# XCiT cross-covariance attention and a GELU feed-forward on one core: a fixed issue order with the next batch's attention between the feed-forward steps

## The chip, the cores and the metric

One Trainium2 chip, one of its cores. The time is the device time of one execution in microseconds (us). Before the change three runs gave 914.15, 913.35 and 912.41 us, a median of 913.35.

## What is computed

The reference normalises q and k of each batch over the 6080 tokens, forms a 256 x 256 matrix of scores between channels, takes the softmax of its rows, and multiplies v by it. The result goes through a feed-forward layer with a tanh GELU, without biases.

```python
B, N, C = (4, 6080, 256)          # d_ff = 2048, all inputs FP32, tau = 1
qn = q / (norm(q, axis=1) + 1e-06)
kn = k / (norm(k, axis=1) + 1e-06)
a  = softmax(kn.transpose(0, 2, 1) @ qn / tau, axis=-1)
x  = (v @ a).reshape(B * N, C)
out = gelu_tanh(x @ w_in) @ w_out
```

## The kernel before, in words

The kernel folds the attention into the first weight: for each batch it computes aw = a @ w_in (256 x 2048, in BF16) and then runs the feed-forward on v itself, so that v @ a is never formed.

A planner orders the instructions of each engine; nothing in the code fixes the order but the order of the calls and the buffers. Set up once (lines 58 to 79): an identity, ones, and w_in and w_out, loaded in FP32 on the SP queue through one staging buffer and converted on ScalarE (L72, L77). v is cast to BF16 by a DMA from DRAM to DRAM on the POOL queue, one DMA of 6080 x 256 for each batch (v_bf, L82), at the head of the batch.

For each of the four batches:

- Gram: 48 tiles of 128 tokens (the last has 64). Each loads q and k with two casting DMAs on POOL (L89, L90; six buffers qk), squares q on ScalarE (L92) and k on VectorE (L93), and adds two matmuls into G, k stationary (L97). The squares of two tiles are added on VectorE (L108), and a matmul with a column of ones sums them over the tokens into ss, one row (L109): 24 for each batch.
- The softmax chain: reciprocal and square root of ss (L118 to L121), small FP32 matmuls that spread the row over the partitions and turn it into a column (L124, L126), scaling and Exp with a row sum (L138, L139), a reciprocal, four transposes of the exponentials on TensorE with copies (L147, L153), and 16 matmuls into awps with eight evictions on ScalarE that give aw (L161, L167).
- Feed-forward, 12 blocks of 512 tokens (the last 448), 48 in all: v arrives transposed by two DMA transposes on SP (vT, L179). For each of 16 chunks of d_ff two matmuls of 512 columns give hp (L187, three buffers of one PSUM bank shared with awps), and ScalarE writes Gelu of it as g (L192). Then, for each of four groups of 128 tokens, 16 matmuls of 256 columns accumulate yp (L199), VectorE copies it out (L203), and the ACT queue stores the block (L207, L214).

The planner already puts the Gram work of a later batch among the feed-forward blocks of the present one where buffers and loads allow, and single yp matmuls between hp matmuls.

Of the kernel before, what the change touches and what calls it, by code (L numbers as in the profile page):

```python
# [2 lines left out]

# [6 lines left out]
FP32 = mybir.dt.float32  # L10
F32R = mybir.dt.float32r
BF16 = mybir.dt.bfloat16
AF = mybir.ActivationFunctionType


@with_exitstack
def kernel(
# [34 lines left out]
    gp = ctx.enter_context(tc.tile_pool(name="gp", bufs=FC + 2))
    yout = ctx.enter_context(tc.tile_pool(name="yout", bufs=3))

    pG = ctx.enter_context(tc.tile_pool(name="pG", bufs=1, space=bass.MemoryType.PSUM))
    pM = ctx.enter_context(tc.tile_pool(name="pM", bufs=1, space=bass.MemoryType.PSUM))
    pH = ctx.enter_context(tc.tile_pool(name="pH", bufs=3, space=bass.MemoryType.PSUM))
    pY = ctx.enter_context(tc.tile_pool(name="pY", bufs=2, space=bass.MemoryType.PSUM))

    ident = const.tile([128, 128], FP32)  # L60
    make_identity(nc, ident)
    ident_bf = const.tile([128, 128], BF16)
    nc.gpsimd.tensor_copy(ident_bf, ident)
    ones_col = const.tile([128, 1], BF16)
    nc.vector.memset(ones_col, 1.0)
    ones_row = const.tile([1, 128], FP32)
    nc.vector.memset(ones_row, 1.0)

    win_st = stage.tile([128, CHUNKS, D], FP32, tag="wst")
    nc.sync.dma_start(out=win_st, in_=moe_w_in.rearrange("(c p) d -> p c d", p=128))  # L70
    win_bf = const.tile([128, CHUNKS, D], BF16)
    nc.scalar.activation(win_bf, win_st, AF.Copy)  # L72

    wout_st = stage.tile([128, FC, 256], FP32, tag="wst")
    nc.sync.dma_start(out=wout_st, in_=moe_w_out.rearrange("(t p) d -> p t d", p=128))
    wout_bf = const.tile([128, FC, 256], BF16)
    nc.scalar.activation(wout_bf, wout_st, AF.Copy)  # L77

    v_bf = dram.tile([B * N, C], BF16)

# [170 lines left out]
```

## Time and profile before

| | |
|---|---|
| median of three runs | 913.35 us |
| span of the profiled execution | 913.5 us |
| TensorE matmuls (PE) busy | 804.7 us, 88% |
| ScalarE (ACT) busy | 503.3 us, 55% |
| VectorE (DVE) busy | 190.3 us, 21% |
| POOL busy | 206.5 us, 23% |
| q and k loads | 376 of 64 KB and 8 of 32 KB, 2.6 us each from issue to landing |
| v casts | 4 of 3040 KB, 20.8 us each |

Busy times overlap, so they don't add up to the span. Sizes of DMAs are those written, in BF16; the FP32 that is read is twice as much. Two matmuls in a row overlap in their recorded times, so the pitch of a run is read from the starts, not from the mean length. The granted clock is 1 at the upper of TensorE's two levels (2.4 GHz) and 0.5 at the lower (1.2 GHz).

### The profile page before, as it was taken

The page shows a single profiled execution, that of the slowest core. Times are in us where ns is not written, and L with a number is a line of the kernel's source. Part 1 is how long each engine was busy: PE and PEld are TensorE (multiplying, and loading weights), DVE is VectorE, ACT ScalarE, POOL GpSimd, SP SyncE. Part 2 cuts the span into 40 slices and gives each one's busy share as a digit, 9 for nine tenths or more (in the row PEclk, how much of TensorE's full clock was granted, in tenths as well). Part 3 has the DMA queues.
Part 4 walks back from the last instruction along what each step waited for, and adds up shares of the span by engine and source line. Part 5 has one row for each costly group of instructions (what it writes and reads, how often), then busy time and mean ns, then how long its engine had stood idle before and what let it go on. Part 6 is the DMA issues. An engine that isn't in the chain of part 4 may idle for free. (4 is left out here: it accounts for less than half of the span.)

```text
span 913.5 us, 13551 instructions
## 1 busy us (share of the span) xinstructions
PE 804.7 (88%) x5136; PEld 498.9 (55%) x5184; DVE 190.3 (21%) x518; ACT 503.3 (55%) x1031; POOL 206.5 (23%) x395
## 2 busy tenths in 40 slices
PE   0537529999999979999999889999999889999998
PEld 0101206666666637575666546575757545766666
DVE  0224302121221322121212313121212210101101
ACT  0333616565656385656566485656565466465563
POOL 2649412221212232312121222312121000000000
PEclk9995659999999989999999989999999999999999
DMA  9999984353534444534444434534443102212111
GB/s 234 232 177 122 187 155 76 82 87 76 81 80 78 85 46 76 96 72 90 73 85 74 90 36 82 92 70 93 70 92 67 55 12 58 58 56 61 46 47 44
DMA packets 134624, 79.80 MB, mean 87 GB/s; under 512 B 58784, under 2 KB 133792, under 8 KB 133792
## 3 DMA queue, kind: packets, MB, share of 16 engines
q0 software_dynamic: 55360, 37.38, 30.3%
q1 hardware_dynamic: 54048, 16.66, 8.2%
q10 hardware_dynamic: 25152, 24.91, 7.9%
q8 instruction: 40, 0.66, 0.3%
q14 instruction: 24, 0.20, 0.1%
HBM read 78.91 MB, written 37.36 MB: 127 GB/s over the span
## 5 line engine op out<-in xcount | busy, mean ns | idle before, releaser
L192 ACT ACTIVATE g<-hp 128x512 bf16<-128x512 f32 (+1 forms) x768 | 384.3, 625 | 275.2 <-PE hp L187 274.7
L199 PE MATMUL yp<-wout_bf,g 128*128 128x256 bf16 (+1 forms) x3072 | 372.8, 273 | 0.1
L187 PE MATMUL hp<-vT,aw 128*128 128x512 bf16 (+1 forms) x1492 | 368.3, 377 | 3.7 <-ACT g L192 1.3
L199 PEld LDWEIGHTS <-g 128*128 128x128 bf16 (+1 forms) x3072 | 300.4, 98 | 68.8 <-issue 0.8
L187 PEld LDWEIGHTS <-aw 128*128 128x128 bf16 x1536 | 148.7, 97 | 159.9 <-issue 35.9
L89 POOL DMA_DIRECT2D qk<-in_q_dram x192 | 111.0, 578 | 449.0 <-ACT g L192 360.9
L97 PE MATMUL G<-qk 128*128 128x256 bf16 (+1 forms) x384 | 79.2, 309 | 65.6 <-DMA qk<-in_k_dram 64.7
L203 DVE COPY ysb<-yp 128x256 f32<-128x256 f32 x192 | 81.2, 423 | 257.3 <-PE yp L199 257.1
L90 POOL DMA_DIRECT2D qk<-in_k_dram x192 | 112.6, 587 | 43.2 <-DMA v_bf<-in_v_dram 39.1
L92 ACT ACTIVATE sq<-qk 128x256 bf16<-128x256 bf16 x192 | 77.0, 455 | 76.9 <-DMA qk<-in_q_dram 54.9
L93 DVE TENSOR_TENSOR sq<-qk 128x256 bf16<-128x256 bf16 x192 | 54.9, 289 | 309.1 <-DMA qk<-in_k_dram 270.5
L97 PEld LDWEIGHTS <-qk 128*128 128x128 bf16 (+1 forms) x384 | 30.5, 101 | 118.3 <-DMA qk<-in_k_dram 94.1
L108 DVE TENSOR_TENSOR sq<-sq 128x512 bf16<-128x512 bf16 x96 | 40.7, 424 | 142.3 <-ACT sq L92 137.7
L109 PE MATMUL ss<-sq,ones_col 128*1 128x512 bf16 x96 | 41.8, 448 | 11.7 <-DVE sq L108 9.9
L167 ACT ACTIVATE aw<-awps,rsinv 128x512 bf16<-128x512 f32 x32 | 19.4, 695 | 9.7 <-PE awps L161 9.7
L161 PE MATMUL awps<-win_bf,eT 128*128 128x512 bf16 x60 | 20.5, 468 | 2.9 <-DVE eT L153 2.9
L124 PE MATMUL M<-rrow,ones_row 1*128 1x256 f32 x8 | 4.9, 710 | 19.7 <-ACT rrow L120 19.7
L109 PEld LDWEIGHTS <-ones_col 128*1 128x1 bf16 x96 | 7.7, 81 | 25.1 <-issue 24.7
L72 ACT ACTIVATE win_bf<-win_st 128x4096 bf16<-128x4096 f32 x1 | 3.6, 3618 | 20.9 <-DMA win_st<-in_moe_w_in_dram 20.9
L118 DVE RECIPROCAL inv<-ss 1x512 f32<-1x512 f32 x4 | 13.4, 3346 | 3.5 <-PE ss L109 3.5
L124 PEld LDWEIGHTS M<-rrow,ones_row 1*128 1x128 f32 x8 | 2.0, 306 | 21.2 <-ACT rrow L120 21.2
L161 PEld LDWEIGHTS <-eT 128*128 128x128 bf16 x64 | 7.1, 117 | 11.3 <-issue 5.5
(27 smaller groups left out, 47.7 us busy)
## 6 DMA issues: line engine op xcount, KB each, us to landing
out_dram<-ysb ACTq DMA_DIRECT2D x44, 512.0 KB, 2.9
v_bf<-in_v_dram POOLq DMA_DIRECT2D x4, 3040.0 KB, 20.8
qk<-in_q_dram POOLq DMA_DIRECT2D x188, 64.0 KB, 2.6
qk<-in_k_dram POOLq DMA_DIRECT2D x188, 64.0 KB, 2.6
win_st<-in_moe_w_in_dram SPq DMA_DIRECT2D x1, 2048.0 KB, 22.2
wout_st<-in_moe_w_out_dram SPq DMA_DIRECT2D x1, 2048.0 KB, 13.6
vT<-v_bf SPq DMA_TRANSPOSE x96, 2.7
out_dram<-ysb ACTq DMA_DIRECT2D x4, 384.0 KB, 2.5
```

What stands on the lines that cost most here:

```text
L89: nc.gpsimd.dma_start(out=qk[:rows, 0, :], in_=q[b, n0 : n0 + rows, :])
L90: nc.gpsimd.dma_start(out=qk[:rows, 1, :], in_=k[b, n0 : n0 + rows, :])
L92: nc.scalar.activation(sq[:rows, 0:256], qk[:rows, 0, :], AF.Square)
L93: nc.vector.tensor_mul(sq[:rows, 256:512], qk[:rows, 1, :], qk[:rows, 1, :])
L97: nc.tensor.matmul(G[:, ci, 0:256], lhsT=qk[:rows, 1, ci * 128 : ci * 128 + 128], rhs=qk[:rows, 0, :], start=first, stop=last,)
L108: nc.vector.tensor_add(sq_prev[:rows], sq_prev[:rows], sq[:rows])
L109: nc.tensor.matmul(ss, lhsT=ones_col, rhs=sq_prev, start=it <= 1, stop=last,)
L161: nc.tensor.matmul(awps, lhsT=eT[:, jc, ic * 128 : ic * 128 + 128], rhs=win_bf[:, jc, fs * 512 : fs * 512 + 512], start=jc == 0, stop=jc = ...
L187: nc.tensor.matmul(hp[:, :cols], lhsT=aw[:, cc, fc * 128 : fc * 128 + 128], rhs=vT[:, cc, :cols], start=cc == 0, stop=cc == CHUNKS - 1)
L192: nc.scalar.activation(g[:, :cols], hp[:, :cols], AF.Gelu_apprx_tanh)
L199: nc.tensor.matmul(yp[:r, 0:256], lhsT=gs[fc][:, s * 128 : s * 128 + r], rhs=wout_bf[:, fc, :], start=fc == 0, stop=fc == FC - 1)
L203: nc.vector.tensor_copy(ysb[:r, s, :], yp[:r, 0:256])
```

## The change

The body of the function is rewritten under a manual schedule: the order of the calls is the order on each engine.

- Loads of q and k take eight rows of tokens for each partition: token p x 47 + r lies on partition p, and one DMA brings rows r0 to r0 + 7 of all partitions, 8 KB in one piece for each of them (load_qk). Batch 0 has seven such chunks, the others six; the 64 tokens left over have a DMA of their own.
- Scores are computed transposed (q stationary), so that their exponentials need no transpose. Square sums of batch 0 go through TensorE with a 128 x 128 matrix of ones (ss_row, one matmul for each row); those of the others are added on VectorE (sum_rows) and summed over the partitions by one FP32 matmul (ss_total). 1/norm is Exp(-0.5 Ln(x)). The sums of the softmax come from matmuls with ones (row_sums).
- w_in and w_out are cast by DMAs on POOL, and stand behind the loads of batch 0; v of batch 0 is cast in two pieces, 1024 tokens behind the fourth pair of loads and the rest behind the weights.
- The feed-forward is software-pipelined over the 48 blocks, in eight steps: step p has four hp matmuls of block n into a pair of PSUM banks, one Gelu of 2 x 512, and eight yp matmuls of block n - 1. Between the steps of block blk of a batch stands the attention of the next batch: loads in blocks 1 to 6, one Gram row for each step in blocks 2 to 7, the cast of v in block 7, the softmax chain in block 8, the eight parts of aw in block 9, evicted by VectorE and ScalarE in turn.
- vT is requested two blocks ahead on SP, and the stores move from the ACT queue to SP.

The lines that are added, cut to the core; the ones removed are those of the kernel above. `ss_row` is `gram_row` with `ones_bf` stationary and the squares moving; `rows_of` lists a chunk's rows.

```diff
+    sqp = ctx.enter_context(tc.tile_pool(name="sqp", bufs=2))
+    vts = ctx.enter_context(tc.tile_pool(name="vts", bufs=4))
+    gp = ctx.enter_context(tc.tile_pool(name="gp", bufs=2))
+    pA = ctx.enter_context(tc.tile_pool(name="pA", bufs=2, space=bass.MemoryType.PSUM))
+    pH = ctx.enter_context(tc.tile_pool(name="pH", bufs=2, space=bass.MemoryType.PSUM))
...
+    def chunks_of(b):
+        sizes = [8, 8, 8, 8, 8, 4, 3] if b == 0 else [8, 8, 8, 8, 8, 7]
...
+    def load_qk(b, c):
+        r0, n = chunks_of(b)[c]
+        last = r0 + n == R
+        qt = qkp.tile([128, 8, 256], BF16, tag="q")
+        kt = qkp.tile([128, 8, 256], BF16, tag="k")
+        for t, src in ((qt, q), (kt, k)):
+            nc.gpsimd.dma_start(
+                out=t[:, 0:n, :],
+                in_=src[b, 0 : R * 128, :].rearrange("(p r) c -> p r c", r=R)[:, r0 : r0 + n, :])
+            if last and REM:
+                nc.gpsimd.dma_start(out=t[:REM, n, :], in_=src[b, R * 128 : N, :])
+        qk_tiles[b, c] = (qt, kt)
...
+    def cast_v(b, t0, t1):
+        nc.gpsimd.dma_start(out=v_bf[b][t0:t1, :], in_=v[b, t0:t1, :])
...
+    def squares(b, c):
+        qt, kt = qk_tiles[b, c]
+        r0, n = chunks_of(b)[c]
+        last = r0 + n == R
+        sq = sqp.tile([128, 8, 512], BF16, tag="sq")
+        if last and REM:
+            nc.gpsimd.memset(sq[:, n, :], 0.0)
+        nc.scalar.activation(sq[:, 0:n, 0:256], qt[:, 0:n, :], AF.Square)
+        nc.vector.tensor_mul(sq[:, 0:n, 256:512], kt[:, 0:n, :], kt[:, 0:n, :])
...
+        SQ[b, c] = sq
+    def sum_rows(b, c):
+        sq = SQ.pop((b, c))
+        a1 = addp.tile([128, 4, 512], BF16, tag="a1")
+        nc.vector.tensor_add(a1, sq[:, 0:4, :], sq[:, 4:8, :])
+        a2 = addp.tile([128, 2, 512], FP32, tag="a2")
+        nc.vector.tensor_add(a2, a1[:, 0:2, :], a1[:, 2:4, :])
+        if c == 0:
+            acc = accp.tile([128, 512], FP32, tag="acc")
+            ACC[b] = acc
+            nc.vector.tensor_add(acc, a2[:, 0, :], a2[:, 1, :])
+        else:
+            acc = ACC[b]
+            a3 = addp.tile([128, 512], FP32, tag="a3")
+            nc.vector.tensor_add(a3, a2[:, 0, :], a2[:, 1, :])
+            nc.vector.tensor_add(acc, acc, a3)
+    def gram_row(b, c, i):
+        if (b, c, i) == (b, 0, 0):
+            G[b] = pA.tile([128, 2, 256], FP32, tag="a", name=f"G{b}")
+        qt, kt = qk_tiles[b, c]
+        rows = rows_of(b, c)
+        r, np_ = rows[i]
+        first = c == 0 and i == 0
+        last = c == len(chunks_of(b)) - 1 and i == len(rows) - 1
+        for jc in range(2):
+            nc.tensor.matmul(
+                G[b][:, jc, :],
+                lhsT=qt[:np_, r, jc * 128 : jc * 128 + 128],
+                rhs=kt[:np_, r, :],
+                start=first and jc == 0, stop=last and jc == 1)
...
+    def ss_total(b):
+        SS[b] = pA.tile([128, 512], FP32, tag="a", name=f"ss{b}")
+        nc.tensor.matmul(SS[b], lhsT=ones_f, rhs=ACC[b], start=True, stop=True)
+    def scores(b):
+        ss = SS[b]
+        lnk = smx.tile([128, 256], FP32, tag="lnk")
+        nc.scalar.activation(lnk, ss[:, 256:512], AF.Ln, bias=eps)
+        qq = smx.tile([128, 2], FP32, tag="qq")
+        for jc in range(2):
+            junk = smx.tile([128, 128], FP32, tag="junk")
+            nc.vector.scalar_tensor_tensor(
+                junk, ss[:, jc * 128 : jc * 128 + 128], 1.0, ident,
+                op0=ALU.mult, op1=ALU.mult, accum_out=qq[:, jc : jc + 1])
+        rk = smx.tile([128, 256], FP32, tag="rk")
+        nc.scalar.activation(rk, lnk, AF.Exp, scale=-0.5)
+        lnq = smx.tile([128, 2], FP32, tag="lnq")
+        nc.scalar.activation(lnq, qq, AF.Ln, bias=eps)
+        rq = smx.tile([128, 2], FP32, tag="rq")
+        nc.scalar.activation(rq, lnq, AF.Exp, scale=-0.5, bias=log_it)
+        S = smx.tile([128, 2, 256], FP32, tag="S")
+        eT = smx.tile([128, 2, 256], BF16, tag="eT")
+        for jc in range(2):
+            nc.vector.tensor_mul(S[:, jc, :], G[b][:, jc, :], rk)
+        for jc in range(2):
+            nc.scalar.activation(eT[:, jc, :], S[:, jc, :], AF.Exp, scale=rq[:, jc : jc + 1])
+        nc.scalar.preload_act_table(AF.Gelu_apprx_tanh)
+        ET[b] = eT
+    def row_sums(b):
+        ps = pA.tile([128, 2], FP32, tag="a")
+        for ic in range(2):
+            for jc in range(2):
+                nc.tensor.matmul(ps[:, ic : ic + 1],
+                                 lhsT=ET[b][:, jc, ic * 128 : ic * 128 + 128],
+                                 rhs=ones_bf[:, 0:1], start=jc == 0, stop=jc == 1)
+        rs = smx.tile([128, 2], FP32, tag="rs")
+        nc.vector.reciprocal(rs, ps)
+        RS[b] = rs
...
+    def aw_part(b, fs, ic, eng):
+        if b not in AW:
+            AW[b] = awp.tile([128, 2, D], BF16, tag="aw", name=f"aw{b}")
+        ps = pA.tile([128, 512], FP32, tag="a")
+        for jc in range(2):
+            nc.tensor.matmul(ps, lhsT=ET[b][:, jc, ic * 128 : ic * 128 + 128],
+                             rhs=win_bf[:, jc, fs * 512 : fs * 512 + 512],
+                             start=jc == 0, stop=jc == 1)
+        o = AW[b][:, ic, fs * 512 : fs * 512 + 512]
+        if eng == "act":
+            nc.scalar.activation(o, ps, AF.Copy, scale=RS[b][:, ic : ic + 1])
+        else:
+            nc.vector.tensor_scalar_mul(o, ps, RS[b][:, ic : ic + 1])
...
+    def mm1(n, p):
+        b = n // NB
+        cols = cols_of(n)
+        if p == 0:
+            GS[n] = gp.tile([128, FC, BLK], BF16, tag="g", name=f"g{n}")
+        hp = pH.tile([128, 2, 512], FP32, tag="h")
+        for u in range(2):
+            fc = 2 * p + u
+            for cc in range(2):
+                nc.tensor.matmul(hp[:, u, :cols],
+                                 lhsT=AW[b][:, cc, fc * 128 : fc * 128 + 128],
+                                 rhs=vt_tiles[n][:, cc, :cols],
+                                 start=cc == 0, stop=cc == 1)
+        nc.scalar.activation(GS[n][:, 2 * p : 2 * p + 2, :cols], hp[:, :, :cols],
+                             AF.Gelu_apprx_tanh)
...
+    def mm2(n, p):
+        cols = cols_of(n)
+        s, half = divmod(p, 2)
+        if half == 0 and s % 2 == 0:
+            YP[n] = pY.tile([128, 2, 256], FP32, tag="y", name=f"yp{n}_{s}")
+            if s == 0:
+                YS[n] = yout.tile([128, 4, 256], FP32, tag="ysb", name=f"ysb{n}")
+        r = min(128, cols - s * 128)
+        yp = YP[n]
+        for fc in range(half * 8, half * 8 + 8):
+            nc.tensor.matmul(yp[:r, s % 2, :],
+                             lhsT=GS[n][:, fc, s * 128 : s * 128 + r],
+                             rhs=wout_bf[:, fc, :], start=fc == 0, stop=fc == FC - 1)
+        if half == 1 and s % 2 == 1:
+            ysb = YS[n]
...
+                nc.vector.tensor_copy(ysb[:, s - 1 : s + 1, :], yp)
...
+        nc.sync.dma_start(
+            out=out[r0 : r0 + nf * 128, :].rearrange("(s p) c -> p s c", p=128),
+            in_=ysb[:, 0:nf, :])
...
+        nch = len(chunks_of(0))
+        VC = 1024
+        for c in range(nch):
+            load_qk(0, c)
+            if c == 3:
+                cast_v(0, 0, VC)
+                load_vt(0)
+            squares(0, c)
+            for i in range(len(rows_of(0, c))):
+                gram_row(0, c, i)
+                ss_row(0, c, i)
+        nc.gpsimd.dma_start(out=win_bf, in_=moe_w_in.rearrange("(c p) d -> p c d", p=128))
+        nc.gpsimd.dma_start(out=wout_bf, in_=moe_w_out.rearrange("(t p) d -> p t d", p=128))
+        cast_v(0, VC, N)
+        load_vt(1)
+        scores(0)
+        row_sums(0)
+        for fs in range(2):
+            aw_part(0, fs, 0, "dve")
+            aw_part(0, fs, 1, "act")
+        NN = B * NB
+        for n in range(NN + 1):
+            b, blk = divmod(n, NB)
+            nxt = b + 1
+            for p in range(PAIRS):
+                if n < NN:
+                    if p == 0 and n + 2 < NN:
+                        load_vt(n + 2)
+                    mm1(n, p)
+                if n == 0 and p in (1, 3):
+                    fs = 2 + p // 2
+                    aw_part(0, fs, 0, "dve")
+                    aw_part(0, fs, 1, "act")
+                if n >= 1:
+                    mm2(n - 1, p)
+                    if p == PAIRS - 1:
+                        store(n - 1)
+                if n < NN and nxt < B:
+                    ncn = len(chunks_of(nxt))
+                    if p == 0 and 1 <= blk <= ncn:
+                        load_qk(nxt, blk - 1)
+                    if p == 0 and blk == ncn + 1:
+                        cast_v(nxt, 0, N)
+                    c = blk - 2
+                    if 0 <= c < ncn:
+                        if p == 0:
+                            squares(nxt, c)
+                        gram_row(nxt, c, p)
+                        if p == 4:
+                            sum_rows(nxt, c)
+                    if blk == 8:
+                        if p == 2:
+                            ss_total(nxt)
+                            scores(nxt)
+                        if p == 6:
+                            row_sums(nxt)
+                    if blk == 9:
+                        aw_part(nxt, p // 2, p % 2, "act" if p % 2 else "dve")
```

## Rows read from the trace of the kernel before

**Rows 1.** The page, busy us, share of the span and instructions of each engine.
```profile
PE 804.7 (88%) x5136; PEld 498.9 (55%) x5184; DVE 190.3 (21%) x518; ACT 503.3 (55%) x1031; POOL 206.5 (23%) x395
```
**Rows 2.** Stages: us, busy of PE, PEld, DVE, ACT, POOL, granted clock, DMA share, GB/s.
```profile
0.00:23.60 23.60, 0.00 (x0) 0.00 (x0) 0.21 (x2) 1.97 (x2) 5.57 (x16) 1.00 0.95 233
23.60:93.80 70.20, 40.41 (x120) 8.51 (x120) 23.98 (x74) 25.95 (x51) 51.21 (x98) 0.83 1.15 175
93.80:131.00 37.20, 11.20 (x44) 5.26 (x45) 7.14 (x17) 14.21 (x25) 7.51 (x15) 0.59 1.00 192
...
310.00:333.00 23.00, 16.63 (x101) 10.22 (x101) 9.64 (x22) 11.65 (x25) 5.29 (x10) 0.85 0.35 54
333.00:520.00 187.00, 185.34 (x1248) 120.44 (x1256) 40.22 (x115) 113.34 (x239) 45.56 (x86) 1.00 0.45 81
520.00:541.00 21.00, 12.95 (x57) 6.09 (x57) 7.68 (x17) 13.33 (x23) 9.36 (x18) 0.76 0.42 51
...
724.00:741.00 17.00, 9.49 (x34) 3.82 (x34) 5.31 (x9) 10.93 (x19) 0.00 (x0) 0.80 0.02 6
741.00:913.50 172.50, 168.20 (x1135) 111.52 (x1145) 20.39 (x48) 95.08 (x192) 0.00 (x0) 1.00 0.18 51
```
**Rows 3.** The chain of waits in time, last batch: start us, length us, what.
```profile
776.37 6.44 PE yp L199 x59
...
790.54 6.44 PE yp L199 x59
...
903.43 6.57 PE yp L199 x59
```
**Rows 4.** Timeline of PE, second batch: start us, length us, line, operation, count.
```profile
334.03 0.82 PE L97 MATMUL G<-qk 128*128 128x256 bf16 x6
...
353.27 1.89 PE L187 MATMUL hp<-vT,aw 128*128 128x512 bf16 x8
355.00 0.27 PE L199 MATMUL yp<-wout_bf,g 128*128 128x256 bf16 x1
355.11 2.48 PE L187 MATMUL hp<-vT,aw 128*128 128x512 bf16 x10
```
**Rows 5.** Timeline of ACT in a block of the last batch.
```profile
769.74 7.46 ACT L192 ACTIVATE g<-hp 128x512 bf16<-128x512 f32 x15
```
**Rows 6.** The page's groups: busy us, mean ns, idle before and releaser.
```profile
L192 ACT ACTIVATE g<-hp 128x512 bf16<-128x512 f32 (+1 forms) x768 | 384.3, 625 | 275.2 <-PE hp L187 274.7
...
L108 DVE TENSOR_TENSOR sq<-sq 128x512 bf16<-128x512 bf16 x96 | 40.7, 424 | 142.3 <-ACT sq L92 137.7
...
L124 PE MATMUL M<-rrow,ones_row 1*128 1x256 f32 x8 | 4.9, 710 | 19.7 <-ACT rrow L120 19.7
...
L72 ACT ACTIVATE win_bf<-win_st 128x4096 bf16<-128x4096 f32 x1 | 3.6, 3618 | 20.9 <-DMA win_st<-in_moe_w_in_dram 20.9
```
**Rows 7.** Timeline of ACT in the first softmax chain.
```profile
97.17 1.28 ACT L120 ACT_TABLE_LOAD   x1
98.46 0.41 ACT L120 ACTIVATE rrow<-inv 1x256 f32<-1x256 f32 x1
```
**Rows 8.** Timeline after the first softmax chain, with idle time before and its releaser.
```profile
103.74 2.34 PE L161 MATMUL awps<-win_bf,eT 128*128 128x512 bf16 x5 [0.72 <-DVE eT L153]
...
130.74 0.53 POOL L90 DMA_DIRECT2D qk<-in_k_dram  x1 [13.69 <-DMA v_bf<-in_v_dram]
...
131.18 1.25 PE L97 MATMUL G<-qk 128*128 128x256 bf16 x4 [19.73 <-DMA qk<-in_k_dram]
```
**Rows 9.** Timeline of POOL's DMA issues in the first batch's Gram.
```profile
42.95 0.54 POOL L82 DMA_DIRECT2D v_bf<-in_v_dram  x1 [0.24 <-DMA qk<-in_q_dram]
...
60.82 0.53 POOL L90 DMA_DIRECT2D qk<-in_k_dram  x1 [8.40 <-DMA v_bf<-in_v_dram]
...
63.48 0.57 POOL L89 DMA_DIRECT2D qk<-in_q_dram  x1
64.00 0.57 POOL L90 DMA_DIRECT2D qk<-in_k_dram  x1
```

More of the change, by code (lines that the diff above doesn't have):

```diff
@@ L2 @@
 from contextlib import ExitStack
+import math
 import concourse.bass as bass
@@ L64 @@
[L64 to L75, printed above, removed]
@@ new lines @@
+    qk_tiles = {}
+    def load_qk(b, c):
[10 more added lines that the diff above has]
+        qk_tiles[b, c] = (qt, kt)
@@ new lines, with load_vt @@
+    v_bf = {}
+    def cast_v(b, t0, t1):
+        nc.gpsimd.dma_start(out=v_bf[b][t0:t1, :], in_=v[b, t0:t1, :])
+    vt_tiles = {}
+    def load_vt(n):
+        b, blk = divmod(n, NB)
+        t0 = blk * BLK
+        cols = min(BLK, N - t0)
+        vT = vts.tile([128, 2, BLK], BF16, tag="vT")
+        for cc in range(2):
+            nc.sync.dma_start_transpose(
+                out=vT[:, cc, :cols], in_=v_bf[b][t0 : t0 + cols, cc * 128 : cc * 128 + 128])
+        vt_tiles[n] = vT
+    G, SS, ACC, SQ = {}, {}, {}, {}
@@ new lines, in rows_of @@
+    def rows_of(b, c):
+        r0, n = chunks_of(b)[c]
+        rows = [(r, 128) for r in range(n)]
+        if r0 + n == R and REM:
+            rows.append((n, REM))
+        return rows
+    def squares(b, c):
+        qt, kt = qk_tiles[b, c]
+        r0, n = chunks_of(b)[c]
+        last = r0 + n == R
[4 more added lines that the diff above has]
+        nc.vector.tensor_mul(sq[:, 0:n, 256:512], kt[:, 0:n, :], kt[:, 0:n, :])
+        if last and REM:
+            nc.scalar.activation(sq[:REM, n, 0:256], qt[:REM, n, :], AF.Square)
+            nc.vector.tensor_mul(sq[:REM, n, 256:512], kt[:REM, n, :], kt[:REM, n, :])
+        SQ[b, c] = sq
@@ new lines, in ss_row @@
+    def ss_row(b, c, i):
+        if (b, c, i) == (b, 0, 0):
+            SS[b] = pA.tile([128, 512], FP32, tag="a", name=f"ss{b}")
+        rows = rows_of(b, c)
+        r, np_ = rows[i]
+        first = c == 0 and i == 0
+        last = c == len(chunks_of(b)) - 1 and i == len(rows) - 1
+        nc.tensor.matmul(SS[b], lhsT=ones_bf[:np_, :], rhs=SQ[b, c][:np_, r, :],
+                         start=first, stop=last)
+    def ss_total(b):
+        SS[b] = pA.tile([128, 512], FP32, tag="a", name=f"ss{b}")
+        nc.tensor.matmul(SS[b], lhsT=ones_f, rhs=ACC[b], start=True, stop=True)
@@ new lines @@
+    ET, RS = {}, {}
+    def scores(b):
[22 more added lines that the diff above has]
+        ET[b] = eT
@@ new lines, with cols_of @@
+    GS = {}
+    def cols_of(n):
+        return min(BLK, N - (n % NB) * BLK)
+    def mm1(n, p):
[6 more added lines that the diff above has]
+            fc = 2 * p + u
+            for cc in range(2):
+                nc.tensor.matmul(hp[:, u, :cols],
[4 more added lines that the diff above has]
+                             AF.Gelu_apprx_tanh)
```

195 lines of the change are left out of this document (47 added, 148 removed).

## The prediction, made before the changed kernel was run

> **What bounds the kernel now.** I read four views, in this order. The page's first line says that TensorE (PE) is busy for 804.7 of 913.5 us, 88% [rows 1]; ScalarE (ACT) and VectorE (DVE) have 55% and 21%, so PE is where to look, and the 12% in which it does nothing. That share is an average over unlike stages, so next the busy times by stage [rows 2], which fall into three kinds. Until 131 us PE does 51.6 us of work (40.41 + 11.20) at a granted clock of 0.83 and then 0.59, while the DMA share is about 1: a start bound by DMA. In the three stages 310 to 333, 520 to 541 and 724 to 741, together 61 us, PE is busy for 39.1 us (16.63 + 12.95 + 9.49) at a clock of 0.76 to 0.85: the softmax chain of a batch, which nothing covers well. In what is left, 913.5 - 131 - 61 = 721.5 us, PE has hardly a hole (185.34 of 187.00 busy, 168.20 of 172.50 in the last batch, clock 1.00): the feed-forward blocks of 512 tokens, with Gram rows of the next batch strewn in. So some 190 us lie outside of dense PE work, and the rest can only be shortened by doing less on PE.
>
> Two durations of dense work are needed. The chain of waits shows 59 matmuls of the second product (yp, 256 columns) in 6.44 us, 0.109 each, and 14.17 us from one such run to the next in the last batch, which has no Gram work beside it [rows 3]. The PE timeline shows eight hp matmuls (512 columns) from 353.27 to 355.00, 0.216 each, then one yp, and hp again 0.11 later; so changing from one product to the other costs nothing by itself [rows 4].
>
> **The change part by part.** The sum is made against the profiled span, 913.5 us, which is the median of the runs (913.35) within 0.02%; nothing is added for what lies around it.
>
> *Dense work.* A full block has 32 hp and 64 yp matmuls, 32 x 0.216 + 64 x 0.109 = 13.9 us; of the 48 blocks 4 have 448 columns in hp (7/8 of 6.92). All hp: 44 x 6.92 + 4 x 6.05 = 329 us; all yp: 48 x 6.99 = 335 us. Together 664, not changed by the edit. The block takes 14.17, 0.26 more than its matmuls. In that block ACT is the pace while hp runs: 15 Gelus of 512 take 7.46 us, 0.497 apart [rows 5], against 0.43 for two hp matmuls, and the planner fills with single yp. The new order puts 8 yp of the block before behind each 4 hp, so a pair of Gelus has 1.74 us of PE time to hide in. One Gelu of 1024 costs 0.497 plus 512 more elements; by the row of the 4096-element conversion (3618 ns) against the 512-element one (625 ns) that is 0.835 ns each [rows 6], so 0.93 us apart, at most 2 x 0.497. ACT then has 8 x 0.93 = 7.4 us of work in 13.9. I keep half of the 0.26 as loss of the many handovers: 47 x 0.13 = 6 us; ends 0 and 12.
>
> *Gram of batches 1 to 3.* 48 rows x 2 matmuls x 0.109 (G alone goes at that pace, six in 0.82 with the last one's tail [rows 4]) x 3 = 31 us, as before, one row per step in blocks 2 to 7. The loads come 14 us ahead. ACT gets one Square of 2048 there, 3.62 - 2048 x 0.835 = 1.9 us, DVE one product and the tree sums. DVE adds 512 bf16 in 424 ns [rows 6]; the product and the tree are 4 + 4 + 2 + 1 + 1 = 12 such pieces, 5.1 us, and 6.8 if the four that write FP32 cost twice as much, in a block of 15.6. Both are covered; with no cover the 18 Squares would cost 18 x 1.9 = 34 us. What goes: 72 of the 96 ss matmuls, 72 x 0.22 = 16 us. What comes: one FP32 ss_total per batch. Its nearest row is the FP32 matmul of 256 columns, which stands as two entries of 0.71 us each at the lower clock [rows 6]: 1.4, at twice the columns 2.8 at most; at the upper clock, and without the tail that each entry has alone, I take 0.9. That is 3 us in three batches (8 at most), with the few columns of row_sums 4.
>
> *aw of batches 1 to 3* moves from the uncovered chain into block 9: 16 x 0.216 x 3 = 10 us of PE, its eviction split between ACT and DVE, hidden.
>
> *The chain itself (block 8).* PE goes on with feed-forward steps; what may stop it is ACT, in order: behind scores() wait the Gelus of the next steps. From the start of step 2: its Gelu ends at 2.1 us, a table load to 3.4 (1.28 [rows 7]), Ln and Exp of 256 to 4.3 (the row of the Sqrt of 256 has 0.41 [rows 7]; 0.45 taken, since these read PSUM or a bias), two small ones beside DVE's product, two Exp to 5.9, the Gelu table to 7.2, the Gelu of step 3 to 8.2. PE with two hp pairs wants that buffer at 6.1 (2 steps of 1.74, the FP32 matmul, one mm1 and mm2 in between). Stall 2.1 us, 6 in all; ends 0 and 5 each. The rows show 1.28 for the load with the next activation 0.01 behind it [rows 7]. The sum goes by that.
>
> *The start.* The old order issues the cast of v (3.1 MB written) ahead of q and k, win and wout in FP32, and 64 KB loads one after another; PE waits 19.73 us at 131 for a k tile queued behind a v cast, as POOL does 13.69 [rows 8]. A v cast alone, 6.2 MB read, runs from 42.95 until POOL is let go at 60.82 [rows 9]: at most 17.9 us, 350 GB/s. Small loads leave POOL every 0.52 us with 131 KB read each, 252 GB/s [rows 9]. The new loads have 1 MB each; I take the v cast's rate, and the small loads' as the slow end. Before the last k row stand 12.45 MB of q and k and 1.05 MB of v: 13.5 MB / 0.35 = 38.5 us, plus 3 (an estimate, by the 2.6 us from issue to landing in the profile's table) = 41 (56 at the slow end). PE's 48 rows of 2 x 256 + 512 columns need 21 us at the upper clock, 41 at the lower (0.43 per 512 columns, as five aw matmuls in 2.34 [rows 8]), so they follow the loads: end of Gram at 44. The scores chain, by the same prices and without a table load, 3.5 to 4 us, 48; win_bf (2.1 MB, next in the queue) lands at 41 + 6 + 1 = 48, too. POOL issues win, wout and the rest of v behind a memset that waits for the ss matmuls of the fifth of seven chunks; these run at about 36 us, before the queue is empty, and if not, the start is later by the difference. Four aw parts at the lower clock, 8 x 0.43 + 0.7 = 4: the first block starts at 52. It has no yp to hide in, ACT sets the pace: 8 x 0.93 + 2 x 0.69 = 9. The second block starts at 61. What is next late there: the transposed v of the third block, wanted at 75, queued on SP behind the cast of the rest of v (win 47, wout 53, rest 68, and 3 more), with the stores behind it on SP; 4 us to spare.
>
> *The end.* The last yp run begins at 903.43 and takes 6.57 [rows 3]; 3.5 us to the span's end, as now.
>
> Sum: 61.5 to the second block, then 664 - 7 (the first block's hp) + 31 + 10 + 4 = 702, 6 for the chains, 6 for handovers, 3.5 at the end: 779; I say 780.
>
> **The rivals.**
> (a) The loads run at the small rate, 252 GB/s: Gram ends 15 us later, 795. For it: the rate of the rows beside a DMA share of 1.15 [rows 2]. Against: these had 0.5 KB written per packet, the new ones have 4 KB in a row.
> (b) Each of the 376 steps loses a tenth of a microsecond as PE goes from one product's semaphores to the other's: +30 less the 6 already taken, 804. For: 0.26 in the old block with only four changes. Against: the 0.11 change in rows 4.
> (c) Ln and Exp are not in one table: five loads instead of two, 3 x 1.28 x 3 = 11.5, 791. The trace shows no Ln. The code names a set with both. The Trainium skill (ScalarE activation tables: per-element evaluation and per-set limits, Table sets in the compiler and the runtime) says that loads are placed for the longest run of functions that one set serves, which would give two; by it (c) falls.
> (d) A table switch costs twice its row, since something that this trace doesn't show must drain around it: 2 x 1.28 x 3 = 7.7 us more behind scores(), 788. Against: 0.01 us between load and activation [rows 7]. The Trainium skill (ScalarE: Activation LUTs, What ACT_TABLE_LOAD costs) gives 2.66 us for a switch, 1.28 of load and 1.38 of drain; by it the sum would be 8 us more. The trace shows the load and not the drain.
> (e) The order of v's casts is tracked by whole tensor: the second block's transpose waits for the whole cast, 71 instead of 61: 790. Against: the second batch's v cast started at 42.95 [rows 9], long before the first batch's last transposes.
> (f) Slower than before: the Gelu pair does not fit its step. With two buffers PE waits as soon as a pair takes longer than 1.74 us from hp to free buffer; each 0.1 beyond costs 37 us over the 376 steps, and 2.1 us gives 780 + 133 = 913. Above 2.1 the change loses. For it: pairs span two PSUM banks, which no row shows, and the fixed order gives PE nothing else to do. Against: 0.93 by the rows, twice 0.497 at most [rows 5].
> (g) The fixed order is no gain: Gram, softmax and start fall out as they do now, 913. Against: nothing in the code leaves the 131 us start as it is.
>
> **How the numbers follow.** Forecast, 760 to 796, with its own bounds (start 8 us earlier, no stalls, no losses; or 12 of loss and 4 at the start): 0.58. (a) 0.09, (b) 0.10, (c) 0.06, (d) 0.05, (e) 0.06, (f) 0.03 at 920 or more, (g) 0.01; faster than 757 0.02. The range 757 to 812 holds the forecast, (a), (c), (d), (e) and most of (b). About 0.2% is what a measurement of this kernel can tell from no change; faster by more 0.96, within it 0.01, slower 0.03.
>
> **What would show it.** First hp matmul at 50 to 55 us; 1 MB loads at about 350 GB/s until 41; Gram blocks of 15.7 us and plain ones of 14; ACT Gelus of 1024 at 0.93 to 1.05; holes in PE only in blocks 8 and of about 2 us; PE above 92% at clock 1.00 after 60 us. Wrong it would be by a start beyond 65 us, by steps longer than 1.85 us, or by ACT as what PE waits for in every step.

## The result, and the profile after

The changed kernel takes 821.81 us (median of four runs, 820.81 to 822.87) against 913.75 of the kernel before beside it: 0.899 of its time, 95% interval 0.897 to 0.901. Faster, as forecast, but 42 us above the 780 and 10 above the range. The profiled execution has a span of 821.1 us; its run took 822.87, so some 1.8 us lie around the span.

First the page's line of the changed kernel that answers to [rows 1]: busy us, share of the span and instructions of each engine.

```profile
PE 756.7 (92%) x5126; PEld 505.5 (62%) x5126; DVE 177.8 (22%) x246; ACT 473.8 (58%) x470; POOL 38.4 (5%) x75
```

By stage, to be laid beside [rows 2]: start and end, us, busy of PE, PEld, DVE, ACT, POOL, granted clock, DMA share, GB/s.

```profile
23.60:50.60 27.00, 16.51 (x85) 8.56 (x84) 6.50 (x14) 8.47 (x12) 7.19 (x12) 0.87 1.01 164
...
60.07:131.00 70.93, 50.58 (x316) 32.63 (x316) 12.51 (x14) 28.45 (x27) 4.28 (x8) 0.83 0.87 171
131.00:389.00 258.00, 250.93 (x1749) 170.93 (x1747) 75.37 (x96) 161.19 (x158) 17.04 (x32) 0.99 0.63 108
389.00:407.00 18.00, 12.09 (x68) 7.06 (x67) 2.01 (x8) 13.97 (x17) 0.00 (x0) 0.81 1.16 204
```

The first hp matmul stands at 50.6 us instead of 109.3, and the stop of 19.73 us until 131 [rows 8] is gone. Then two kinds of stage remain in which PE is not dense: the 71 us from 60 on, with 20 us of holes at a clock of 0.83, and the softmax chain at 389, with 6 us of holes and a clock of 0.81. The changed kernel's waits of PE name both (us in total, times, longest):

```profile
PE hp L243 <- DMA vT<-vbf: 21.4, 4, 9.3
PE hp L243 <- ACT g L247: 18.2, 5, 5.9
```

The start-to-start time of a block's first hp matmul shows what each costs. A plain block takes 13.89 us, one with Gram rows 15.64, one with aw 17.35: the matmuls and nothing else. But blocks 1, 2 and 3 take 19.32, 28.01 and 24.05 (13.89, 15.64 and 15.64 without a wait: 26.2 too many, of which 20.4 are the waits below and most of the rest matmuls at the lower clock behind them; a wait at the first hp of a block counts to the block before), and the three blocks with a softmax chain take 23.07, 23.09 and 23.83.

**The first kind: v arrives late.** Timeline of PE in the changed kernel: start us, length us, line, operation, count, idle before and its releaser.

```profile
79.38 0.61 PE L243 MATMUL hp<-vT,aw 128*128 128x512 bf16 x1 [5.27 <-DMA vT<-vbf]
89.33 1.44 PE L243 MATMUL hp<-vT,aw 128*128 128x512 bf16 x3 [9.34 <-DMA vT<-vbf]
...
113.52 1.44 PE L243 MATMUL hp<-vT,aw 128*128 128x512 bf16 x3 [5.75 <-DMA vT<-vbf]
```

POOL's timeline shows what the transposes of v meet:

```profile
41.56 0.57 POOL L79 DMA_DIRECT2D qt<-in_q_dram  x1
...
64.83 0.53 POOL L79 DMA_DIRECT2D kt<-in_k_dram  x1 [11.42 <-DMA vbf<-in_v_dram]
...
84.27 0.54 POOL L89 DMA_DIRECT2D vbf<-in_v_dram  x1 [2.17 <-DMA qt<-in_q_dram]
156.83 0.53 POOL L119 MEMSET sq<- 128x512 bf16 x1 [72.02 <-DVE a L131]
...
196.93 0.53 POOL L89 DMA_DIRECT2D vbf<-in_v_dram  x1
```

The code puts the next batch's loads into blocks 1 to 6 and its v cast into block 7. POOL does not wait for blocks: it issues the first load at 41.6 us, before the first block, the last in block 2, and the whole v cast of batch 1 at 84.3. Batch 2's v cast goes out at 196.9, still in batch 0. Buffers and landings stop it, and once in each batch the memset of the last square buffer, which VectorE has to give back first (72.02 us at 156.83); so it runs ahead by a batch at most. From 65 to 95 us the queues have this (packets, MB written, share of the 16 engines; then the issues with the median us to landing):

```profile
q0 software_dynamic: 1735, 5.87, 97.8%
q1 hardware_dynamic: 1536, 0.38, 9.9%
...
vT<-vbf SPq DMA_TRANSPOSE x5, 28.5
```

q0 carries POOL's casting loads, q1 the transposes and stores of SP. The number of packets is nearly the same; the bytes stand at 15 to 1. A load's packet of 4096 B takes 0.32 us, a v cast's of 24,320 B 1.81 us, a transpose's of 256 B 0.018 us (medians over the packets). SP's timeline has a pair of transposes that takes 26 us beside the long packets, and one that takes 2.9 behind them:

```profile
86.98 25.95 SPq L99 DMA_TRANSPOSE vT<-vbf  x2
...
113.65 2.92 SPq L99 DMA_TRANSPOSE vT<-vbf  x2
```

That each small packet waits out a long one is what these counts suggest; e4 and e5 below test it.

**The second kind: five table loads in the chain.** Timeline of ACT in the second chain of the changed kernel:

```profile
389.87 1.02 ACT L247 ACTIVATE g<-hp 128x1024 bf16<-128x1024 f32 x1 [0.71 <-PE hp L243]
390.91 1.28 ACT L179 ACT_TABLE_LOAD   x1
392.20 0.47 ACT L179 ACTIVATE lnk<-ss,eps 128x256 f32<-128x256 f32 x1
392.70 1.28 ACT L187 ACT_TABLE_LOAD   x1
393.99 0.42 ACT L187 ACTIVATE rk<-lnk 128x256 f32<-128x256 f32 x1
394.43 1.28 ACT L189 ACT_TABLE_LOAD   x1
...
396.03 1.28 ACT L191 ACT_TABLE_LOAD   x1
...
398.58 1.28 ACT L198 ACT_TABLE_LOAD   x1
399.87 1.94 ACT L247 ACTIVATE g<-hp 128x1024 bf16<-128x1024 f32 x2
```

Each Ln and each Exp in turn has a load of its own, and PE stands still for 5.91 us:

```profile
400.95 1.86 PE L243 MATMUL hp<-vT,aw 128*128 128x512 bf16 x4 [5.91 <-ACT g L247]
402.61 1.91 PE L263 MATMUL yp<-wout_bf,g 128*128 128x256 bf16 x8
```

The first matmuls behind the hole take 1.86 and 1.91 us instead of 1.03: they run at the lower of the two levels. In the first batch, where the kernel names the table set ahead of the chain, only the load of Gelu is there.

### The profile page after: what moved, and what is told of

Its sections match the earlier page's. It is cut to its first block, busy times and chain, and to the rows that moved or that the text cites. A ratio compares the mean times of both kernels' runs of the same rounds, so it can differ in the third digit from the quotient of the medians.

```text
span 821.1 us, 11523 instructions
## 1 busy us (share of the span) xinstructions
PE 756.7 (92%) x5126; PEld 505.5 (62%) x5126; DVE 177.8 (22%) x246; ACT 473.8 (58%) x470; POOL 38.4 (5%) x75
## 4 chain that ended last, share of the span: by engine, by line
PE 79%; DMA 16%; ACT 2%; SPq 1%; issue 0%; POOL 0%; DVE 0%; DVEq 0%; POOLq 0%
PE yp L263 37%; PE hp L243 36%; DMA vT<-vbf 9%; PE G L153 4%; DMA vbf<-in_v_dram 3%; DMA kt<-in_k_dram 2%; SPq L99 1%; DMA qt<-in_q_dram 1%; PE ps L219 1%; ACT g L247 1%; PE ss L166 0%; ACT L198 0%; ACT L189 0%; ACT L187 0%; ACT L179 0%
## 5 line engine op out<-in xcount | busy, mean ns | idle before, releaser
L247 ACT ACTIVATE g<-hp 128x1024 bf16<-128x1024 f32 (+1 forms) x384 | 388.9, 1015 | 298.5 <-PE hp L243 296.8
L243 PE MATMUL hp<-vT,aw 128*128 128x512 bf16 (+1 forms) x1536 | 398.4, 383 | 39.7 <-DMA vT<-vbf 21.4
L263 PE MATMUL yp<-wout_bf,g 128*128 128x256 bf16 (+1 forms) x3072 | 402.0, 275 | 0.0
L269 DVE COPY ysb<-yp 128x512 f32<-128x512 f32 x92 | 63.6, 691 | 481.2 <-PE yp L263 481.2
L153 PE MATMUL G<-kt,qt 128*128 128x256 bf16 (+1 forms) x384 | 76.6, 282 | 12.9 <-DMA kt<-in_k_dram 12.9
L120 ACT ACTIVATE sq<-qt 128x2048 bf16<-128x2048 bf16 (+3 forms) x25 | 45.0, 1801 | 26.0 <-DMA qt<-in_q_dram 13.4
L153 PEld LDWEIGHTS <-qt 128*128 128x128 bf16 (+1 forms) x384 | 38.5, 101 | 25.5 <-issue 10.2
L121 DVE TENSOR_TENSOR sq<-kt 128x2048 bf16<-128x2048 bf16 (+3 forms) x25 | 28.9, 1154 | 30.7 <-DMA kt<-in_k_dram 28.0
L133 DVE TENSOR_TENSOR a<-a 128x1024 f32<-128x1024 bf16 x18 | 22.0, 1225 | 0.6
L131 DVE TENSOR_TENSOR a<-sq 128x2048 bf16<-128x2048 bf16 x18 | 21.9, 1215 | 0.0
L79 POOL DMA_DIRECT2D qt<-in_q_dram x25 | 13.9, 554 | 80.6 <-ACT g L247 59.0
L79 POOL DMA_DIRECT2D kt<-in_k_dram x25 | 13.8, 553 | 25.2 <-DMA vbf<-in_v_dram 11.4
L142 DVE TENSOR_TENSOR acc<-acc,a 128x512 f32<-128x512 f32 x15 | 10.4, 692 | 0.5
L141 DVE TENSOR_TENSOR a<-a 128x512 f32<-128x512 f32 x15 | 10.4, 692 | 0.5
## 6 DMA issues: line engine op xcount, KB each, us to landing
qt<-in_q_dram POOLq DMA_DIRECT2D x20, 512.0 KB, 14.5
```

Of the source, the lines that this page charges most:

```text
L79: nc.gpsimd.dma_start(out=t[:, 0:n, :], in_=src[b, 0 : R * 128, :].rearrange("(p r) c -> p r c", r=R)[:, r0 : r0 + n, :])
L120: nc.scalar.activation(sq[:, 0:n, 0:256], qt[:, 0:n, :], AF.Square)
L121: nc.vector.tensor_mul(sq[:, 0:n, 256:512], kt[:, 0:n, :], kt[:, 0:n, :])
L131: nc.vector.tensor_add(a1, sq[:, 0:4, :], sq[:, 4:8, :])
L133: nc.vector.tensor_add(a2, a1[:, 0:2, :], a1[:, 2:4, :])
L153: nc.tensor.matmul(G[b][:, jc, :], lhsT=qt[:np_, r, jc * 128 : jc * 128 + 128], rhs=kt[:np_, r, :], start=first and jc == 0, stop=last and ...
```

## The experiments

All are compared with the kernel before, which took 915 to 916 us beside them. "Block 8" is the block with the softmax chain, one for each of batches 1 to 3; 15.02 us without a hole (17.19 measured with one of 2.17).

**Pace POOL** (e1). Theory: the loads run ahead of their blocks and starve the transposes. Rival: v of batch 0 is simply cast too late. POOL gets a copy of one element of block n's Gelu output ahead of each load pair and v cast of that block, so that it can't run ahead.

```diff
+    def gate(n):
+        gt = smx.tile([1, 1], BF16, tag="gate")
+        nc.gpsimd.tensor_copy(gt, GS[n][0:1, 0, 0:1])
...
+                        gate(n)
                         load_qk(nxt, blk - 1)
...
+                        gate(n)
                         cast_v(nxt, 0, N)
```

> POOL is held back: ahead of each load_qk of the next batch, and of its cast_v, POOL copies one element of the present block's first Gelu, so that the DMA can't be issued before that block. Theory 'run-ahead' (POOL issues all of batch 1's loads and its v cast between 41 and 84 us, and the transposes of v, with their small packets, share the DMA engines with them): the 26.2 us that blocks 1 to 3 take beyond their matmuls fall to 0 to 4, total 795 to 800. Rival 'late data' (the blocks wait for the rest of batch 0's v cast and three transposes, whatever else runs): the 26 stay, 821.

797.83 us, 0.872 of before (0.868 to 0.876). Blocks 1 to 3 fell to 13.89, 15.64 and 15.64: the whole 26 us are gone there, and late data as a cause with them. (The four times lie between 793.68 and 801.37, and these blocks are those of the fastest, so the 24.0 between the medians is the rougher figure.) POOL is now held, and q0's packets in the same 65 to 95 us are a third:

```profile
62.43 0.18 POOL L95 COPY gt<-g 1x1 bf16<-1x1 bf16 x1 [20.69 <-ACT g L251]
62.66 0.55 POOL L79 DMA_DIRECT2D qt<-in_q_dram  x1
63.20 0.54 POOL L79 DMA_DIRECT2D kt<-in_k_dram  x1
76.38 0.18 POOL L95 COPY gt<-g 1x1 bf16<-1x1 bf16 x1 [12.64 <-ACT g L251]
```

```profile
q0 software_dynamic: 593, 2.17, 43.7%
q1 hardware_dynamic: 4866, 1.97, 35.0%
```

**Name the table set** (e2) and **both edits** (e3).

```diff
         ss = SS[b]
+        if b > 0:
+            nc.scalar.preload_act_table_set("natural_log_exp_and_others")
         lnk = smx.tile([128, 256], FP32, tag="lnk")
```

> The table set with both Ln and Exp is named ahead of scores() in batches 1 to 3, too, so that two table loads are left of five. Theory 'loads and clock' (three loads of 1.28 us, and a stall so long that the clock falls to its lower level behind it): block 8's excess over its matmuls falls from 7.9 to 2 to 2.5, 17 us in all, 804. Rival 'loads alone': 3 x 3.85 = 11.5 us, 810. Rival 'ACT is not what block 8 waits for': 821.

> Both edits. If the two losses are independent, their gains add: 'run-ahead' with 'loads and clock' gives 776 to 781, which would be the time forecast; 'late data' with 'loads and clock' 804. If the faster chain brings the next loads forward into a new collision, the sum is missed by more than 4 us.

e2: 813.65 us, 0.887 (0.880 to 0.894), a gain of only 8.2. Its three blocks 8 did what they should (18.87, 17.19, 17.19), 16.7 us less in all; but block 10 of batch 0 grew from 14.16 to 22.19:

```profile
236.76 1.44 PE L245 MATMUL hp<-vT,aw 128*128 128x512 bf16 x3 [6.11 <-DMA vT<-vbf]
```

The shorter chain brings these transposes forward against batch 2's v cast, which POOL had issued at 196.8 us. Half of the gain was turned into a wait for the same queue. That seems to hang on timing: one of the four executions took 804.62 us, the 804 expected, the profiled one 812.77. With both edits nothing of that is left: e3 takes 781.32 us, 0.854 (0.852 to 0.856), 40.5 less than the changed kernel, while the single edits gave 24.0 and 8.2. In the profile of e3 the chain has one load at each end, and a hole of the size that the prediction had worked out (2.1):

```profile
359.36 1.28 ACT L183 ACT_TABLE_LOAD   x1
360.66 0.47 ACT L185 ACTIVATE lnk<-ss,eps 128x256 f32<-128x256 f32 x1
...
363.29 1.28 ACT L204 ACT_TABLE_LOAD   x1
364.58 1.94 ACT L253 ACTIVATE g<-hp 128x1024 bf16<-128x1024 f32 x2
```

```profile
365.66 1.02 PE L249 MATMUL hp<-vT,aw 128*128 128x512 bf16 x4 [2.17 <-ACT g L253]
```

**Shorter pieces, same bytes** (e4, e5). If the long packets are what starves the transposes, loads of the same size in shorter pieces let them through without any pacing. e4 gives partition p the tokens r x 128 + p, so that each DMA writes eight pieces of 512 B for each partition instead of one of 4096; e5 writes two of 2048.

```diff
-                in_=src[b, 0 : R * 128, :].rearrange("(p r) c -> p r c", r=R)[:, r0 : r0 + n, :])
+                in_=src[b, r0 * 128 : (r0 + n) * 128, :].rearrange("(r p) c -> p r c", p=128))
```

```diff
+            for i in range(0, n, 4):
...
+                        nc.gpsimd.dma_start(
+                            out=t[:, 0:8, :].rearrange("p (g r) c -> p g r c", g=2),
+                            in_=src[b, r0 * 128 : (r0 + 8) * 128, :].rearrange(
+                                "(g p r) c -> p g r c", g=2, r=4))
```

> Same DMAs of 1 MB read for q and k, but token r x 128 + p lies on partition p, so that each partition reads eight pieces of 1 KB in place of one of 8 KB. Nothing else changes; POOL runs ahead as before. Theory 'packets' (the engines alternate between queues packet by packet, so that a queue with large packets starves one with small ones): the excess of blocks 1 to 3 falls from 26 to under 10. Rival 'bytes' (what counts is the amount of traffic ahead): it stays at 26 or grows. For the start: if small pieces are what held the old loads to 252 GB/s, Gram ends at 50 to 56 us in place of 42 and the total is 8 to 14 us worse; if the old rate was POOL's issue pace, Gram ends at 42 to 45.

> The changed kernel with q and k read in pieces of 4 KB (four token rows for a partition) in place of 8 KB; POOL runs ahead as before, and nothing else changes. Theory 'packets': beside loads of 8 KB pieces the trace shows 1735 packets of the loads and 1536 of the transposes in 30 us, nearly one to one, and one of 4096 B written takes 0.32 us; the pair of transposes of a block has some 63 packets for each engine, so it takes 63 x (0.32 + 0.03) = 22 us beside 8 KB pieces, some 12 beside 4 KB pieces and 5 beside 1 KB pieces, against 15.6 that a block lasts. The excess of blocks 1 to 3 falls from 26 to 2 to 8, total 798 to 806. Theory 'bytes': 26 stays. A third, that only the 1 KB pieces' slower issue on POOL helped (0.9 us in place of 0.54 each): 26 stays, since POOL is as fast here as with 8 KB.

e4: 797.92 us, 0.872 (0.870 to 0.874), the same as pacing. Blocks 1 to 3 have no wait, although POOL runs ahead as in the changed kernel (v cast at 95.4). The cast, whose packets the edit does not shorten, still delayed transposes, by up to 17.4 us from issue to landing, but none that PE was waiting for. Queues of e4 from 69 to 95 us:

```profile
q0 software_dynamic: 7213, 3.64, 104.7%
q1 hardware_dynamic: 3792, 1.31, 34.5%
```

A packet of q0 now takes 0.06 us, and in less time q1 moves 1.31 MB instead of 0.38. The short pieces cost 4 us at the start (first hp at 54.9 instead of 50.6, Gram to 46 instead of 42), a quarter of rival (a)'s 15: between the two cases of the expectation, and nearer to the one by which POOL's issue held the old loads back.

e5: 814.95 us, 0.889 (0.886 to 0.893), 9 above the expectation. Start to start, blocks 1 to 4 take 15.0, 23.1, 28.1 and 17.0. Blocks 1 and 2 keep 8.5 us too many instead of 17.8, so shorter packets do help; but blocks 3 and 4 have 13.8, where the expectation gave 2 to 8 for all. The first hp of block 4 waits for its transposes, which met the v cast that went out at 92.2 us with packets as long as before:

```profile
127.14 1.89 PE L253 MATMUL hp<-vT,aw 128*128 128x512 bf16 x4 [12.28 <-DMA vT<-vbf]
```

So a load's place among the blocks matters as much as its pieces.

**Pace only the v cast** (e6): the gate of e1 ahead of cast_v alone.

```diff
+                        gate(n)
                         cast_v(nxt, 0, N)
```

> Of the two gates only the one ahead of the next batch's v cast is set; the loads of q and k run ahead as in the changed kernel. If the loads' packets starve the transposes, the waits of blocks 1 and 2 (5.4 and 12.4 us) stay and at most the 8.4 of block 3, which falls into the cast, goes: excess 15 to 19. If the v cast with its still larger packets is the cause, all 26 go.

811.37 us, 0.886 (0.884 to 0.888): 10.4 us of e1's 24. Block 3 is free of its wait; the two waits behind the q and k loads stay, 14.5 us. Both kinds of transfer starve the transposes.

**Three table loads instead of five** (e7): e1 with both Ln ahead of both Exp.

```diff
-        rk = smx.tile([128, 256], FP32, tag="rk")
-        nc.scalar.activation(rk, lnk, AF.Exp, scale=-0.5)
         lnq = smx.tile([128, 2], FP32, tag="lnq")
         nc.scalar.activation(lnq, qq, AF.Ln, bias=eps)
+        rk = smx.tile([128, 256], FP32, tag="rk")
+        nc.scalar.activation(rk, lnk, AF.Exp, scale=-0.5)
```

> POOL held back as in e1_gate, and in scores() the two Ln stand together ahead of the two Exp, without a named set: three table loads in place of five. e1_gate has 22.4 to 23.5 us for block 8, e3_both with two loads 17.2 to 18.9. If every load costs its 1.28 us and no more: 22.6 - 2 x 1.28 = 20.0. If a longer hole also costs some us at the lower clock behind it: between 18.5 and 20, nearer to the upper end. If the loads don't matter: 22.6. Total 788 to 791 by the first two.

791.65 us, 0.864 (0.863 to 0.866). PE's longest hole is 5.91 us with five loads, 4.09 with three, 2.17 with two: 0.91 and 1.92 a load, on either side of the 1.28 that a load takes. The edit is not only two loads less: with the two Ln together the chain waits for a product on VectorE twice, 0.95 us that e3 does not have (timeline of ACT in e7):

```profile
368.21 0.30 ACT L191 ACTIVATE lnq<-qq,eps 128x2 f32<-128x2 f32 x1 [0.58 <-DVE junk L187]
...
370.78 0.91 ACT L201 ACTIVATE eT<-S,rq 128x256 bf16<-128x256 f32 x2 [0.37 <-DVE S L199]
```

Block 8 takes 20.4 to 21.9 us instead of the 20.0 or less expected. The medians fall by 6.2 us from e1 to e7 and by 10.3 from e7 to e3, the spans of the profiled executions by 1.7 and 11.7, since e1's is the fastest of its four; 5.5 and 5.8 us are the holes of the three blocks. What the second step has beyond that is in the profiled executions 2.5 us less at the lower clock behind the holes (the mean granted clock of the three is 0.982, 0.983 and 0.989) and 2.2 us in which a k tile came late in e7. So these runs show a load's share of the hole, and not a price of it in the whole time.

**What the sums on VectorE are worth** (e8): e3 with the square sums of batches 1 to 3 on PE, one ss matmul for each row, without sum_rows and ss_total.

```diff
-                        if p == 4:
-                            sum_rows(nxt, c)
+                        if p >= 2:
+                            ss_row(nxt, c, p - 2)
+                        if p == 7:
+                            ss_row(nxt, c, 6)
+                            ss_row(nxt, c, 7)
...
-                            ss_total(nxt)
```

> e3_both with one part undone: the square sums of batches 1 to 3 go through TensorE again, one matmul of 512 columns for each row in place of the sums on VectorE and the FP32 matmul. The dense stages have no idle TensorE time, so each of 144 matmuls should cost its 0.216 us: + 31, less 3 x 0.9 for the FP32 matmul = + 28, 809. If the old kernel's idle time of 0.2 around each ss matmul comes with it: + 55, 836. If something other than TensorE sets the pace of a step: no change, 781.

813.91 us, 0.888 (0.885 to 0.891), 32.6 above e3. A Gram block goes from 15.64 to 17.37: eight more matmuls of 512 columns in a block that PE paces, 8 x 0.216 = 1.73. So the move to VectorE is worth some 31 us. The 28 expected, with 3 x 0.9 taken off for the FP32 matmul, was too low: without that matmul PE only waits longer for ACT in block 8, 3.03 us instead of 2.17.

**The start** (e9, e10). e9 puts batch 0's v cast ahead of its q and k loads, as the old kernel has it; e10 leaves out the memset in batch 0, which waits for PE and has the weights' loads behind it on POOL.

```diff
+        cast_v(0, 0, VC)
+        cast_v(0, VC, N)
+        load_vt(0)
         for c in range(nch):
             load_qk(0, c)
-            if c == 3:
-                cast_v(0, 0, VC)
-                load_vt(0)
...
-        cast_v(0, VC, N)
```

```diff
-        if last and REM:
+        if last and REM and b > 0:
             nc.gpsimd.memset(sq[:, n, :], 0.0)
```

> What is tried: the placing of batch 0's v cast behind the Gram loads. Edit: e3_both with both pieces of batch 0's v cast ahead of the first q and k loads, as the old kernel had it (nothing left out). If the start is bound by the bytes that stand in the queue before the last k row, the 5.2 MB more of them at 350 GB/s move the end of the first Gram from about 42 us to 57 and the first hp matmul from 50.6 to about 65: 781 + 14 = 795 us, 792 to 798. If the loads and the cast run beside each other, or the later blocks of batch 0 win something from an earlier v, the first hp stands below 58 and the time below 789.

> What is tried: the one wait of POOL in the start. Edit: e3_both without the memset of the unused square rows in batch 0, where nothing reads them (no result changes). In the changed kernel POOL waited 11.6 us at the memset for ss matmuls, the weights' loads behind it were issued at 40 us, and win landed at 47.3 us, where TensorE had waited 2.2 us for it. If that wait is what is late last, win lands 4 to 5 us earlier, the first hp stands at 48 to 49 instead of 50.6, and the time is about 779 us (778 to 780), a gain of 0.2 to 0.4%. If the scores chain is late last, the first hp stays at 50 to 51 and the time within 1 us of e3_both.

e9: 792.54 us, 0.867 (0.864 to 0.870); the first hp stands at 62.6, 11.8 later than e3's, for 15 worked out from 350 GB/s: 5.2 MB in 11.8 us are 440 GB/s. The place of the cast is worth 11 us.

e10: 777.07 us, 0.849 (0.847 to 0.851), the fastest, and 1 below the 778 to 780 expected. POOL issues win at 29.4 us instead of e3's 39.3, PE no longer waits for it, and the first hp stands at 47.8 instead of 50.9 (timelines of POOL and of PE in e10):

```profile
29.36 0.73 POOL L323 DMA_DIRECT2D win_bf<-in_moe_w_in_dram  x1 [1.92 <-DMA qt<-in_q_dram]
```

```profile
47.77 3.14 PE L249 MATMUL hp<-vT,aw 128*128 128x512 bf16 x8
```

1.1 us of the three are given back in the first block (10.71 for 9.56). In the profiled executions the other 3.4 us of e10's gain over e3 are two blocks 8 of 17.19 instead of 18.87, without the lower clock; so of the 4.2 us between the medians perhaps only 2 are the memset's, as in the profiled executions.

## Why the prediction was wrong, point by point

The 42 us between the changed kernel's span and the sum: +26.2 in blocks 1 to 3, +18.6 in the three blocks 8 (24.9 for 6.3), -6 for handovers that cost nothing, -1.4 at the second block's start, +1 at the end, and 4 in small excesses, 0.4 in the first block of each later batch among them. e3 takes the two large terms back and comes out at 781.3, with a span of 778.5 against the sum's 779. That it comes so near is in part luck: the 6 us that the handovers did not cost are nearly made up by 3.4 at the lower clock in two blocks 8, by the end and by the small excesses.

Two slips of the prediction's arithmetic change no verdict: a tenth of a microsecond in each of 376 steps is 38 us and not 30, so rival (b) stood at 812, the edge of the range; and the sum starts from 61.5 where the working has 61.

**The failed step: "The loads come 14 us ahead", and "4 us to spare" for v.** I read the code's order as POOL's pace. [rows 9] show POOL's issue held by landings, never by a block, and the changed kernel has nothing in blocks 1 to 6 that would: six pairs of buffers of 1 MB read each, which POOL fills as fast as earlier transfers land. I then took the transposes at the 3 us of a quiet queue. The cast of v's rest landed 64.5 us (68 in the sum), so data was early; the pair of transposes behind it landed after 15 and 23 us instead of 3. No rival and no sign of being wrong named these transposes; the nearest, (e), was about the cast. e1 shows the run-ahead, e4 the long packets as what makes it harmful, e6 that loads and cast share in it. [rows 8] held a warning: a k tile that PE awaited for 19.73 us with a v cast ahead of it. I priced that for the old start and not for the transposes. The nearly equal packet counts of the two queues agree, if the packets of the trace are those of the page, which no run shows, with the Trainium skill (DMA: Bandwidth & Descriptors, section Queues, rings and completion order), which says that each DMA engine goes round the queues that have work for it packet by packet; by that rule a queue of small packets gets a share of the bytes as small as they are.

**The failed assumption: two table loads.** Rival (c), at 0.06, came true: five. Its price was too low as well. 3 x 1.28 x 3 = 11.5 us are in the holes (5.91 - 2.1, three times, 11.4), but 7.2 more come from the lower clock behind a hole of six us. The Trainium skill (ScalarE activation tables: per-element evaluation and per-set limits, Table sets in the compiler and the runtime) speaks of the longest run that one set serves; this trace does not agree: Ln and Exp in turn had a load each, although one named set serves both, as e2 shows. I used a page's rule against a rival where the code held the evidence for it: batch 0 names the set and the others don't.

**Right.** The dense work: 13.89 for 13.9 forecast, 15.64 for 15.7. The Gelu of a pair hides in its step (mean in the changed kernel 1015 ns, between 0.93 and 1.05), so rival (f) has no ground, and PE does not wait for it outside of the chains and the first block:

```profile
L247 ACT ACTIVATE g<-hp 128x1024 bf16<-128x1024 f32 (+1 forms) x384 | 388.9, 1015 | 298.5 <-PE hp L243 296.8
```

Rival (a) fell: the new loads ran faster than forecast (below), and pieces as short as the old ones cost 4 us in e4, not 15. The FP32 ss_total takes 0.87 for 0.9. VectorE's product and tree need 1.22 + 1.22 + 1.23 + 0.69 + 0.69 = 5.1 us a block, the lower of the two forecasts, off the path. The chain's hole with two loads is 2.17 for 2.1. Rival (d), a drain around each load, fell: the rows of ACT above have 0.01 to 0.03 us on either side of a load. The Trainium skill's 1.38 us of drain (ScalarE: Activation LUTs, What ACT_TABLE_LOAD costs) stands in none of them. Rival (e) fell: the second block started at 60.1 without a wait for v.

**Right by compensation.** The start: first hp at 50.6 for 52. The loads were faster than the 350 GB/s taken; from 5 to 20 us the DMAs write some 212 GB/s, which is 424 read:

```profile
10.00:15.00 5.00, 4.65 (x16) 2.39 (x17) 1.25 (x2) 1.91 (x1) 1.05 (x2) 1.00 1.06 212
```

But the kt of the fifth chunk was waited for until 32.3, the 16 rows from there on ran in part at the lower level, the Gram ended at 42 (44), and the memset that the prediction had named let win go only at 39.1. Handovers between the products: half of 0.26 was charged 47 times, 6 us; no block shows any, so rival (b) fell, too. That the old 0.26 came from ACT's pace alone is argued, not shown.

## What to carry over

A place in the code paces a transfer only if its engine waits for something there: ask of each DMA engine what stops it, and if nothing does, give it a wait on the work it belongs to. Small packets beside a queue of long ones got their share here by the packet and not by the byte, so the latency of a quiet queue is no price for a busy one. And where two faults share a path, judge the cure of one with the other cured as well: here the table set gave 8 us alone and 17 behind the pacing.

## What the runs showed of the hardware that I had not expected

- The engines served a queue of 4096 B packets (0.32 us each) and one of 256 B packets (0.018 us) nearly packet for packet, 1735 to 1536. A transpose went from 2.6 us at best to 40.6 at worst from issue to landing (5.8 at worst in the kernel before); with 512 B packets in the loads the worst was 17.4.
- Loads of 8 KB read in one piece for each partition read 424 GB/s together, and in pieces of 1 KB (e4) still 394; the 131 KB loads of before left POOL at 252 [rows 9].
- When PE runs at the lower level behind a hole is not settled. Behind 5.91 us block 8 had the lower level in all three batches; behind 2.17 us in two of three in e3's profile (18.87, 17.19, 18.86), in one in e2's and in none in e9's and e10's (17.19 each), with the same work in it. The hole's length alone does not say which, and the cause stays open.
